# Four operand differences of the last layer: from VectorE to ScalarE sign changes and adding transfers of GpSimd's queue

## The chip, the cores and the metric

The kernel runs on one core of one Trainium2 chip. The metric is the device time in microseconds (us) of one execution, the median of several runs. Engines are named as in the profile: PE is TensorE, DVE is VectorE, ACT is ScalarE, POOL is GpSimd, SP is SyncE, which issues most transfers.

## The reference, cut to what matters

Attention with a tanh cap, then a gated layer (silu), then a second layer with two matrices and a leaky activation. The change lies in the last matrix product.

```
attn = softmax(cap * tanh(q k^T / 8 / cap));  x = attn v      # 2 x 12 heads, 448 rows, 64 wide
xn  = x / rms(x) * rms_g
x   = (silu(xn @ w_gate) * (xn @ w_val)) @ w_out               # 768 -> 1536 -> 768
h   = x @ w_in                                                  # 768 -> 2048
g   = max(h, 0) + alpha * min(h, 0)
out = g @ w_out2                                                # 2048 -> 768, 896 tokens
```

## The kernel before, in words

Every fp32 product is made of three passes over split operands: a number is its rounded high part plus a rest, and PE multiplies high by high, high by low and low by high. A high part is a CAST on ACT (line 133 for weights, line 1187 for the last layer's operands), a low part a subtraction on DVE (line 139 for weights, line 619 through the helper `tt` for operands).

The layers run as blocks of 2 x 2 matrices with Winograd's seven products in place of eight, so that sums and differences of blocks are needed on both sides. In the last layer the inner dimension of 2048 is cut in two. The first half (8 pieces `fh`, `fl`) is multiplied plainly, by the units `c`. The second half is a 2 x 2 block matrix with the quarters B11, B12 (in the buffer `zt[2]`, printed as `b_3496`) and B21, B22 (`zt[3]`, printed as `b_3669`), and goes through the seven products of `LONG`, by the units `f`. Four of its operands are differences, each made in place, in two halves h = 0 and 1 of 128 x 896 elements:

- T1 = B12 - B11, in the place of B11, the operand of product P5;
- T2 = B22 - T1, in the place of T1, the operand of P6;
- T3 = B22 - B12, in the place of B12, the operand of P7;
- T4 = B21 - T2, in the place of T2, the operand of P4.

PE's work is a list of slots of 18 matmuls each. From `f0`, the first slot of the last layer, they are: 8 slots of `c`, then two slots each of P1, P5, P6, P7, P4, then 8 slots of `c` for the other half of the output rows, then two slots each of P3 and P2. So P5 has the slots 10 and 11 after f0, P6 12 and 13, P7 14 and 15, P4 16 and 17; the first slot of a product uses half 0 of its operand, the second half 1. PSUM holds two banks of sums: P1 and P6 write the pair of tiles printed x and m, P5 and P7 the pair printed s.

All work of other engines hangs on slots: `do(n, rank, fn, ...)` puts it behind slot n, and `rank` orders it there. That gives the order of each engine's instructions and no time: an engine runs ahead as far as its waits allow. ACT and DVE run here about one slot ahead of the slot that their work is hung on. Per slot there is a weight unit's high part on ACT (rank 0) and its low part on DVE (rank 2), hung two slots before its use. Its buffer is one of four (`wh`, `wl`), so ACT's cast of a unit waits until PE is through with the unit four before. The raw weights come by SP's queue, three buffers in turn; the next load goes out when DVE has combined (line 118) what came before.

`fsplit` (line 1187) makes the high part of an operand half on ACT, `fsplit_low` its rest on DVE, and `t_sum` a difference on DVE. `keep` (line 1225) copies PSUM sums to SBUF on ACT and `plus` adds them on DVE. The tables that hang all of these on slots are

```
for n, (p, b, at_) in enumerate(zip(LONG, (B11, B11, B11, B12, B11, B22, B21), (4, 7, 10, 12, 14, 20, 22))):
for n, abc in ((6, (B11, B12, B11)), (9, (B11, B22, B11)), (11, (B12, B22, B12)), (12, (B11, B21, B11))):
```

Every operand half goes through the same places: a difference, its high part, its rest, then PE.

Of the kernel before, what the change touches and what calls it, by code (L numbers as in the profile page):

```python
# [13 lines left out]
AF = mybir.ActivationFunctionType  # L14
ALU = mybir.AluOpType
# [42 lines left out]
def attn_moe_kernel(ctx: ExitStack, tc: tile.TileContext, units, qk_in, v, sel, w, gvec, alpha, out):  # L58
    nc = tc.nc
# [354 lines left out]
    with tc.manual_schedule():  # L414
# [203 lines left out]
        def tt(out, a, b, op):  # L618
            nc.vector.tensor_tensor(out=out, in0=a, in1=b, op=op)  # L619
# [70 lines left out]
        def do(n, rank, fn, *a):  # L690
            hooks.setdefault(n, []).append((rank, len(hooks[n]) if n in hooks else 0, fn, a))
# [65 lines left out]
        LONG = ("P1", "P5", "P6", "P7", "P4", "P3", "P2")  # L757
# [125 lines left out]
        f0 = at_of["c", 0, 0, 0]  # L883
# [45 lines left out]
        for g in range(G1):  # L929
            at_ = {p: at_of.get(("g", g, p)) for p in STEADY}  # L930
# [209 lines left out]
        for g in range(G2):  # L1140
            at_ = {p: at_of["z", g, p] for p in STEADY}
# [31 lines left out]
        for k in range(KC):  # L1173
            n = f0 + (-3, -3, -2, -2, 0, 0, 2, 2)[k]
# [3 lines left out]
        B11, B12, B21, B22 = ((2, 0), (2, 1), (3, 0), (3, 1))  # L1178

        def quarter(b, h):  # L1180
            c = b[1] + 4 * h
            return zt[b[0]][:, c:c + 3:2]
# [8 lines left out]
            ls[h] = place(14 + n % 2 * 4 + h)  # L1191
            tt(ls[h], quarter(b, h), hs[h], ALU.subtract)

        def t_sum(out, a, b, h):
            tt(quarter(out, h), quarter(a, h), quarter(b, h), ALU.subtract)

        for n, (p, b, at_) in enumerate(zip(LONG, (B11, B11, B11, B12, B11, B22, B21), (4, 7, 10, 12, 14, 20, 22))):
            for h in range(2):
                do(f0 + at_ + h, 5, fsplit, n, p, b, h)
                do(f0 + at_ + 1 + h, 2, fsplit_low, n, p, b, h)  # L1200
        for n, abc in ((6, (B11, B12, B11)), (9, (B11, B22, B11)), (11, (B12, B22, B12)), (12, (B11, B21, B11))):
            for h in range(2):
                do(f0 + n, 3.5, t_sum, *abc, h)

        def parts_of(i):
            return (fb[i][0][:, :, :S], slice(0, 2)), (fb[i][1][:, :1, :S], slice(2, 3))
# [139 lines left out]
```

## Time and profile before

| what | value |
|---|---|
| median of 3 runs | 552.24 us (552.23 to 552.39) |
| the profiled execution's own time | 552.85 us |
| its span | 551.1 us |
| PE busy | 545.6 us, 99% of the span |
| DVE, ACT, POOL busy | 448.5, 370.6, 98.8 us |
| last layer, from f0 to PE's last matmul | 438.24 to 547.46 us |

The span is what the trace covers, 1.75 us less than the execution's own time. A start time in the rows below is counted from the start of the span. Ends of matmuls are modelled, so PE's row of busy time says that it is fed, not that it is at its peak.

### The profile page before, as it was taken

The numbers are of one execution on the slowest core, as the hardware profiler recorded it, in microseconds if no ns is written. First come the engines' busy times: TensorE is split into PE (matmuls) and PEld (weight loads), VectorE is DVE, ScalarE is ACT, GpSimd is POOL, SyncE is SP. The second block draws the span as 40 slices with busy tenths as digits, with TensorE's granted clock in tenths as the row PEclk, the third lists the DMA queues.
The fourth block names the chain that finished last, engine by engine and source line by source line (L and its number), as shares of the span: only waits on it lengthen the run. The fifth ranks groups of instructions, "written<-read, shape, count | busy, mean of one in ns | idle before, by whom it ended". The sixth has DMA issues, their size and how long they took to land.

```text
span 551.1 us, 7691 instructions
## 1 busy us (share of the span) xinstructions
PE 545.6 (99%) x3061; PEld 461.3 (84%) x3061; DVE 448.5 (81%) x511; ACT 370.6 (67%) x433; POOL 98.8 (18%) x54
## 2 busy tenths in 40 slices
PE   8999999999999999999999999999999999999997
PEld 5444544699999999999999999999999999999996
DVE  4698889898999967878889898979866899999242
ACT  7989999477766554576757554787967996467110
POOL 0034663300065231010000048101111000000000
PEclk9999999999999999999999999999999999999999
DMA  7756420400334534065510573005512267013022
GB/s 253 260 188 197 164 73 8 163 12 1 120 120 162 178 110 171 1 228 173 184 46 1 229 230 114 1 0 173 172 58 69 105 203 255 0 59 115 0 101 100
DMA packets 17316, 66.09 MB, mean 120 GB/s; under 512 B 3584, under 2 KB 5504, under 8 KB 17280
## 3 DMA queue, kind: packets, MB, share of 16 engines
q1 hardware_dynamic: 16746, 65.08, 34.9%
q8 instruction: 24, 0.39, 0.3%
q10 hardware_dynamic: 390, 0.39, 0.2%
q0 software_dynamic: 144, 0.13, 0.1%
q14 instruction: 12, 0.10, 0.1%
HBM read 62.66 MB, written 2.75 MB: 119 GB/s over the span
## 4 chain that ended last, share of the span: by engine, by line
PE 96%; DVE 1%; ACT 1%; DMA 1%; issue 0%; DVEq 0%
PE s L395 19%; PE x L395 13%; PE m L395 13%; PE s L775 9%; PE s L749 8%; PE x L775 7%; PE oo L236 6%; PE s L207 5%; PE x L749 4%; PE m L775 4%; PE rps L249 3%; PE m L749 2%; PE s L408 1%; PE m L408 1%; PE x L408 1%; ACT pt L221 1%
## 5 line engine op out<-in xcount | busy, mean ns | idle before, releaser
L133 ACT CAST wh<-wt 128x768 fp32r<-128x768 f32 x105 | 87.1, 832 | 66.4 <-PE s L775 24.9
L139 DVE TENSOR_TENSOR wl<-wt,wh 128x768 fp32r<-128x768 f32 x108 | 113.6, 1053 | 12.5 <-ACT wh L133 12.2
L126 POOL TENSOR_TENSOR wt<-wt 128x768 f32<-128x768 f32 x33 | 75.1, 2284 | 265.9 <-DVE wt L118 97.9
L113 ACT CAST top<-raw 128x768 f16<-128x768 bf16 x64 | 68.8, 1076 | 27.0 <-DMA raw<-w_in 11.7
L118 DVE SCALAR_TENSOR_TENSOR wt<-raw,top 128x768 uint32<-128x768 uint32 x68 | 69.8, 1028 | 1.5 <-ACT top L113 1.5
L395 PE MATMUL s<-xx,wh 128*128 128x448 f32 x264 | 63.5, 364 | 0.0
L395 PEld LDWEIGHTS s<-xx,wh 128*128 128x128 f32 x264 | 49.4, 187 | 4.6 <-issue 0.7
L395 PE MATMUL x<-xx,wh 128*128 128x448 f32 x204 | 49.9, 366 | 0.0
L395 PE MATMUL m<-xx,wh 128*128 128x448 f32 x204 | 49.5, 364 | 0.0
L619 DVE TENSOR_TENSOR xx<-b,xx 128x896 fp32r<-128x896 f32 (+1 forms) x40 | 48.8, 1228 | 0.6 <-ACT xx L632 0.6
L216 ACT ACTIVATE pt<-s,cinv 128x896 f32<-128x896 f32 (+1 forms) x48 | 41.1, 911 | 6.2 <-PE s L207 5.9
L395 PEld LDWEIGHTS x<-xx,wh 128*128 128x128 f32 x204 | 38.2, 188 | 3.5 <-issue 0.4
L395 PEld LDWEIGHTS m<-xx,wh 128*128 128x128 f32 x204 | 38.2, 187 | 3.0
L775 PE MATMUL s<-xx,wh 128*128 128x448 f32 x132 | 40.0, 362 | 0.0
L236 PE MATMUL oo<-pt,vt 128*32 128x448 f32 x384 | 38.5, 540 | 0.4 <-ACT pt L221 0.3
L221 ACT ACTIVATE pt<-pt,cap_t 128x3136 f32<-128x3136 f32 (+2 forms) x13 | 35.3, 2714 | 0.4
L395 PE MATMUL s<-xx,wl 128*128 128x448 f32 x132 | 33.8, 364 | 0.0
L236 PEld LDWEIGHTS oo<-pt,vt 128*32 128x32 f32 x384 | 12.2, 110 | 23.6 <-issue 21.4
L775 PE MATMUL x<-xx,wh 128*128 128x448 f32 x104 | 31.2, 362 | 0.0
L749 PE MATMUL s<-xx,wh 128*128 128x448 f32 x96 | 27.2, 364 | 0.0
L775 PEld LDWEIGHTS s<-xx,wh 128*128 128x128 f32 x132 | 24.7, 187 | 2.1
L775 PE MATMUL s<-xx,wl 128*128 128x448 f32 x72 | 26.5, 367 | 0.0
(223 smaller groups left out, 1119.0 us busy)
## 6 DMA issues: line engine op xcount, KB each, us to landing
raw<-w_in SPq DMA_DIRECT2D x68, 768.0 KB
rw<-qk_in SPq DMA_DIRECT2D x11, 480.0 KB
vt<-v_in SPq DMA_DIRECT2D x12, 256.0 KB
out<-b SPq DMA_DIRECT2D x2, 448.0 KB
out<-b SPq DMA_DIRECT2D x2, 224.0 KB
out<-e SPq DMA_DIRECT2D x1, 448.0 KB
out<-c SPq DMA_DIRECT2D x2, 224.0 KB
gt<-us SPq DMA_DIRECT2D x23, 3.5 KB
```

The source lines that it names most:

```text
L113: copy(top_of[u].bitcast(F16)[:, 1::2], raw_t[u].bitcast(BF16)[:, 4:4 * n + 4:4])
L118: nc.vector.scalar_tensor_tensor(out=f_t[u].bitcast(U32), in0=raw_t.pop(u).bitcast(U32)[:, 1:2 * n + 1:2], scalar=13, in1=top_of.pop(u), o ...
L126: add(out=t, in0=f_t[a], in1=f_t[b], op=op)
L133: copy(h_t[u], f_t[u].rearrange("p (k m) -> p k m", m=P))
L139: nc.vector.tensor_tensor(out=l_t[u], in0=f_t[u].rearrange("p (k m) -> p k m", m=P), in1=h_t[u], op=ALU.subtract)
L216: nc.scalar.activation(out=t[:, 2 * g:2 * g + w], in_=st.pop((i, g))[:, :w, :S], func=AF.Tanh, scale=cinv)
L221: nc.scalar.activation(out=t[:, done:to], in_=t[:, done:to], func=AF.Exp, scale=cap_t)
L236: nc.tensor.matmul(oo[i][q * Q:q * Q + Q, :S], vv[:, n, q % 2 * Q:q % 2 * Q + Q], t[:, min(n, TILES - 1), :], start=c == 0, stop=c == TG, ...
L395: nc.tensor.matmul(ps[:, r, c0:c1], lhs, rhs[:, c0:c1], start=first and n == 0, stop=n == len(mm) - 1, skip_group_check=True,)
L619: nc.vector.tensor_tensor(out=out, in0=a, in1=b, op=op)
L749: nc.tensor.matmul(dst[m], wt[:, kk * MB + m, :], x, start=first and u == 0 and kk == 0 and n == 0, stop=u == 1 and kk == 1 and n == 2, sk ...
L775: nc.tensor.matmul(dst[m], wt[:, kk * MB + m, :], x, start=start and ks + kk == 0 and i == 0, stop=fin and last and kk == 1 and i == 2, sk ...
```

## The change

The function that makes a difference no longer subtracts on DVE. ACT changes the sign of the quarter in place, and a transfer of POOL's queue adds the other quarter to it in SBUF. The order of operations is changed with it: T3 is made before T2, the halves of T2 and T4 are hung on two slots in turn, and the splits of P5 and P6 are hung one slot later, P6's at a low rank.

```
-        def t_sum(out, a, b, h):
-            tt(quarter(out, h), quarter(a, h), quarter(b, h), ALU.subtract)
-
-        for n, (p, b, at_) in enumerate(zip(LONG, (B11, B11, B11, B12, B11, B22, B21), (4, 7, 10, 12, 14, 20, 22))):
+        def t_sum(b, a, h):
+            q = quarter(b, h)
+            nc.scalar.activation(out=q, in_=q, func=AF.Copy, scale=-1.0)
+            nc.gpsimd.dma_start(out=q, in_=quarter(a, h), accum_op=ALU.add)
+
+        for n, (p, b, at_) in enumerate(zip(LONG, (B11, B11, B11, B12, B11, B22, B21), (4, 8, 11, 12, 14, 20, 22))):
             for h in range(2):
-                do(f0 + at_ + h, 5, fsplit, n, p, b, h)
-                do(f0 + at_ + 1 + h, 2, fsplit_low, n, p, b, h)
-        for n, abc in ((6, (B11, B12, B11)), (9, (B11, B22, B11)), (11, (B12, B22, B12)), (12, (B11, B21, B11))):
+                do(f0 + at_ + h, 5 if p != "P6" else 0.7, fsplit, n, p, b, h)
+                do(f0 + at_ + (p != "P6") + h, 2, fsplit_low, n, p, b, h)
+        for n, step, b, a in ((6, 0, B11, B12), (8, 0, B12, B22), (9, 1, B11, B22), (12, 1, B11, B21)):
             for h in range(2):
-                do(f0 + n, 3.5, t_sum, *abc, h)
+                do(f0 + n + step * h, 3.5, t_sum, b, a, h)
```

On ACT, from the copies of the first `c` sums (slot 6, tiles x and m) to the copies of P5's sums (`e`), the order before is:

```order
L1225 COPY c_4122<-x 128x896
L1225 COPY c_4123<-m 128x448
L133 CAST wh<-wt 128x768
L1187 CAST xx<-b_3496 128x896
L133 CAST wh<-wt 128x768
L1225 COPY b_4172<-s 128x896
L1225 COPY b_4172<-s 128x448
L133 CAST wh<-wt 128x768
L1187 CAST xx<-b_3496 128x896
L133 CAST wh<-wt 128x768
L1187 CAST xx<-b_3496 128x896
L133 CAST wh<-wt 128x768
```

In the changed kernel the same stretch of ACT, after the same copies, is (line 1196 is the sign change; the first pair is of T3, the single ones are the halves of T2; line 1187 makes the high parts, here of P5's two halves and P6's first):

```order
L1196 ACTIVATE b_3496<-b_3496 128x2x448 x2
L1187 CAST xx<-b_3496 128x896
L133 CAST wh<-wt 128x768
L1227 COPY b_4175<-s 128x896
L1227 COPY b_4175<-s 128x448
L1196 ACTIVATE b_3496<-b_3496 128x2x448
L1187 CAST xx<-b_3496 128x896
L133 CAST wh<-wt 128x768
L1196 ACTIVATE b_3496<-b_3496 128x2x448
L133 CAST wh<-wt 128x768
L1187 CAST xx<-b_3496 128x896
L133 CAST wh<-wt 128x768
```

Four sign changes have come into the stretch, and P5's high parts stand behind T3's sign changes. T1's two sign changes stand earlier, before the copies.

On DVE the piece from P1's second low part (the first row) to P5's second low part reads as follows before, with T1's difference as the row `x2` of b_3496 alone:

```order
L619 TENSOR_TENSOR xx<-b_3496,xx 128x896
L118 SCALAR_TENSOR_TENSOR wt<-raw,top_94 128x768
L619 TENSOR_TENSOR b_3496<-b_3496 128x2x448 x2
L139 TENSOR_TENSOR wl<-wt,wh 128x768
L118 SCALAR_TENSOR_TENSOR wt<-raw,top_95 128x768
L126 TENSOR_TENSOR wt<-wt 128x768
L139 TENSOR_TENSOR wl<-wt,wh 128x768
L619 TENSOR_TENSOR xx<-b_3496,xx 128x896
L126 TENSOR_TENSOR wt<-wt 128x768
L139 TENSOR_TENSOR wl<-wt,wh 128x768
L619 TENSOR_TENSOR xx<-b_3496,xx 128x896
```

In the changed kernel the same piece of DVE, from the same row, is:

```order
L619 TENSOR_TENSOR xx<-b_3496,xx 128x896
L118 SCALAR_TENSOR_TENSOR wt<-raw,top_94 128x768
L139 TENSOR_TENSOR wl<-wt,wh 128x768
L118 SCALAR_TENSOR_TENSOR wt<-raw,top_95 128x768
L126 TENSOR_TENSOR wt<-wt 128x768
L139 TENSOR_TENSOR wl<-wt,wh 128x768
L126 TENSOR_TENSOR wt<-wt 128x768
L139 TENSOR_TENSOR wl<-wt,wh 128x768
L619 TENSOR_TENSOR xx<-b_3496,xx 128x896
L126 TENSOR_TENSOR wt<-wt 128x768
L139 TENSOR_TENSOR wl<-wt,wh 128x768
L619 TENSOR_TENSOR xx<-b_3496,xx 128x896
```

The difference is gone, and P5's low parts stand one weight unit later than before: each now stands behind the low part of a unit (line 139) that it stood ahead of.

## Rows read from the trace of the kernel before

**Rows 1.** Busy time by stretch: us; then PE, PEld, DVE, ACT, POOL, granted clock, DMA.

```profile
460.00:470.00 10.00, 10.00 (x51) 9.28 (x50) 9.79 (x12) 7.52 (x10) 0.00 (x0) 1.00 0.51 175
470.00:480.00 10.00, 10.00 (x51) 9.26 (x51) 10.00 (x13) 4.20 (x5) 0.00 (x0) 1.00 0.00 0
480.00:490.00 10.00, 10.00 (x51) 9.28 (x50) 10.00 (x12) 7.29 (x10) 0.00 (x0) 1.00 0.01 2
```

**Rows 2.** Chain that ended last, in order of time: start, us, what.

```profile
474.64 7.28 PE s L775 x36
481.92 1.21 PE x L775 x6
...
485.56 2.43 PE x L775 x12
...
540.16 7.29 PE s L775 x36
547.46 0.02 issue
547.48 0.39 DVE c L619
```

**Rows 3.** Timeline of DVE: start, us, line, operation, tiles.

```profile
458.38 1.09 DVE L619 TENSOR_TENSOR xx<-b,xx 128x896 fp32r<-128x896 f32 x1
459.38 0.95 DVE L118 SCALAR_TENSOR_TENSOR wt<-raw,top 128x768 uint32<-128x768 uint32 x1
460.25 2.09 DVE L619 TENSOR_TENSOR b<-b 128x896 f32<-128x896 f32 x2
462.25 0.95 DVE L139 TENSOR_TENSOR wl<-wt,wh 128x768 fp32r<-128x768 f32 x1
...
474.55 1.08 DVE L619 TENSOR_TENSOR c<-x,c 128x896 f32<-128x896 f32 x1
475.55 0.62 DVE L619 TENSOR_TENSOR c<-m,c 128x448 f32<-128x448 f32 x1
...
476.95 1.08 DVE L619 TENSOR_TENSOR xx<-b,xx 128x896 fp32r<-128x896 f32 x1
...
481.69 1.08 DVE L619 TENSOR_TENSOR xx<-b,xx 128x896 fp32r<-128x896 f32 x1
```

**Rows 4.** Timeline of ACT, the idle time before a row and its releaser in brackets.

```profile
443.97 0.94 ACT L1126 ACTIVATE zn<-b 128x896 f32<-128x896 f32 x1
...
457.37 1.08 ACT L113 CAST top<-raw 128x768 f16<-128x768 bf16 x1
460.42 0.83 ACT L133 CAST wh<-wt 128x768 fp32r<-128x768 f32 x1 [1.97 <-DVE wt L118]
...
462.10 0.94 ACT L1187 CAST xx<-b 128x896 fp32r<-128x896 f32 x1
...
467.19 0.84 ACT L133 CAST wh<-wt 128x768 fp32r<-128x768 f32 x1 [1.33 <-PE s L775]
467.93 1.33 ACT L1225 COPY b<-s 128x896 f32<-128x896 f32 x2
```

**Rows 5.** Timeline of SP's queue: issue of one weight load.

```profile
460.36 0.33 SPq L102 DMA_DIRECT2D raw<-w_in  x1
```

**Rows 6.** Busy time by us in which that load moves; columns as in rows 1.

```profile
461.00:462.00 1.00, 1.00 (x7) 0.93 (x6) 1.00 (x2) 1.00 (x2) 0.00 (x0) 1.00 0.83 123
462.00:463.00 1.00, 1.00 (x7) 0.92 (x6) 1.00 (x2) 1.00 (x3) 0.00 (x0) 1.00 0.87 338
463.00:464.00 1.00, 1.00 (x7) 0.93 (x6) 1.00 (x2) 1.00 (x3) 0.00 (x0) 1.00 0.77 320
```

**Rows 7.** DMA issues: line, count, KB each, median us to landing.

```profile
raw<-w_in SPq DMA_DIRECT2D x68, 768.0 KB
...
sel_t<-sel_in POOLq DMA_DIRECT2D x1, 128.0 KB, 4.8
```

**Rows 8.** Timeline of POOL: its only transfer.

```profile
1.22 0.72 POOL L436 DMA_DIRECT2D sel_t<-sel_in  x1 [0.78 <-POOLq L1336]
```

## The prediction

> **What bounds the kernel now.** I read first the busy time by stretch, to see which engine leaves no gap. In the 30 us in which the four differences are made, PE is busy 10.00 of every 10 us and its granted clock is 1.00; DVE has 9.79 to 10.00, ACT 4.20 to 7.52, POOL nothing, and the DMA engines are idle from 470 on [rows 1]. Next I read the chain that ended last, in order of time: from P5's first slot at 474.64 it is matmuls without a break, slot behind slot of 3.64 us (P5's 36 matmuls take 7.28), to 547.46, and then DVE's last sums and the output [rows 2]. So PE bounds, and a full DVE beside it costs nothing as long as operands come in time. A matmul is not slowed by DVE either: the last 36, at 540.16, with DVE nearly out of work, take 7.29 us against 7.28 for the 36 at 474.64 [rows 2].
>
> From this follows the sign: work taken from DVE here can give next to nothing, while an operand that comes late stops PE and is paid in full. The question is the slack of the operands. Before, P6's low parts end at 476.95 + 1.08 = 478.03 and 481.69 + 1.08 = 482.77 [rows 3]; its slots start at 481.92 and 485.56 [rows 2]. That is 3.9 and 2.8 us, and 3.64 us is one slot.
>
> **The change, part by part.** Removed from DVE: eight subtractions, of which two take 2.09 us [rows 3], so 8 x 1.04 = 8.4 us. DVE is not the bound: 0 us at the end of the program. Added to ACT: eight sign changes. The nearest row is an ACTIVATE of the same 128 x 896, 0.94 us [rows 4], so 7.5 us. ACT has 2.5 us and more idle in each 10 [rows 1], so by itself 0 as well. Added to POOL's queue: eight transfers of 448 KB. POOL has no other work then, so nothing is queued behind them there. What can cost is the time that each transfer stands between two steps of a chain.
>
> The chain starts with T1. Its first sign change can follow ACT's cast at 457.37 + 1.08 = 458.45 and ends at 459.4. The second overwrites what P1's second low part reads, which ends at 458.38 + 1.09 = 459.47, so it ends at 460.4. Before, ACT sat idle 1.97 us there, until 460.42 [rows 3, 4]; this is hidden.
>
> Call X the time at which T1's second half has landed. ACT's next step is T3's sign changes, in place on B12, which T1's transfers read: they have to wait for these, half by half. Behind the second on ACT stand P5's first high part, a weight cast, a copy of sums, T2's sign change and the rest. From rows of 0.94 (sign change, and high part), 0.84 (weight cast), 0.95 (a unit's low part on DVE) and 1.08 (an operand's) [rows 3, 4]: T3's second sign change, P5's first high part and the cast are through at X + 2.7. DVE's low part of that unit and P5's low part: X + 4.75. T2's first sign change: X + 5.7. P5's second high part and a cast: X + 7.5. DVE again two low parts: X + 9.5. T2's second sign change: X + 10.4. DVE meanwhile has a weight sum (0.95), P1's two sums (1.08 and 0.62 [rows 3]), one unit's low part (0.95) and then P6's first low part (1.08): X + 14.2. Rows that follow each other on an engine overlap by 0.08 us (459.38 + 0.95 is 460.33, and the next starts at 460.25 [rows 3]); for about ten of them that is 0.8, so X + 13.4. PE needs that part one matmul, 0.20 us (7.28 / 36), after 481.92. **No stall as long as X is at most 482.1 - 13.4 = 468.7.** P6's second half: sign change done at X + 10, transfer, high part and low part (2.0), needed at 485.8; with 4.2 us for a transfer by itself (below) that allows X = 469.6. T4's halves have some two us more, and weights are cast three slots ahead, so the first limit decides.
>
> Now X. The trace has no adding transfer and none from SBUF to SBUF. Nearest row: a weight load of 768 KB. One issued at 460.36 moves in the next three us, with 0.83 + 0.87 + 0.77 = 2.5 us of all DMA engines [rows 5 to 7]. By its bytes 448 KB takes 1.44 us if the added operand is all that counts, and 2.9 if goal and operand are both read. POOL's row for a transfer is 0.72 us [rows 8], and the load starts some 0.6 us after its issue [rows 5, 6], so a transfer alone takes 2.8 to 4.2 us. T1's pair doesn't move alone: it starts at 459.4 + 0.72 + 0.6 = 460.7, and that load and the one behind it move in the same stretch (175 GB/s over 10 us from 460 is 1.75 MB, two loads and a rest [rows 1]). With half of the engines each, a pair of 2.9 us lands at 460.7 + 5.8 = 466.5; a pair of 5.8 us, last after both loads, at 460.7 + 5.8 + 5.0 = 471.5. The outer ends are a pair at the load's rate with nobody beside it, X = 463.6, and the other transfer of POOL's queue, 128 KB in 4.8 us [rows 7], taken by its bytes: 3.5 x 4.8 = 16.8 us for one, which puts X at 494 and some 25 us on the program. I hold to the load, whose size is nearer, since the 128 KB are loaded in the program's first us together with the first operands. Between 466.5 and 471.5 I take the middle, X = 469.0, so 0.3 us of stall, with 0 and 2.8 as its ends.
>
> The page "Collectives: The Full Stack" of the Trainium skill, section "The bandwidth ceiling: the fold count and why AG ≠ RS ≠ AR", says that an adding transfer is slower because it has two sources to read through one ring, not because of the addition (measured ratio 1.93). No run here shows it yet; by it the pair would take 5.6 us and X be about 471.3, the first rival's case.
>
> **The sum.** The profiled execution took 552.85, its span 551.1. Minus 8.4 on DVE and plus 7.5 on ACT count 0, since PE's row has no gap for either; the stall adds 0.3: 553.15 for an execution like the profiled one, which lies 0.6 above the median of 552.24. For the median: 552.24 + 0.3 = **552.5 us**. A difference under about 0.2%, 1.1 us, can't be told from none here, so this is "the same".
>
> **Rivals.**
> First, slower by two reads beside the loads: X = 471.5. T3's and P5's parts follow it at once, P6's first low part is through at 484.9 against 482.1, and PE stalls 2.8 us before P6's first slot: 555.0. For it: the DMA engines are busy there half of the 10 us, and more in the us of a load [rows 1, 6]. Against it: they have the other half, and two queues may fill each other's gaps. It decides from X = 469.8 on, which is 1.1 us of stall.
> Second, an addition that is slower still, 4.4 us a transfer, half again as long as two reads. X is then about 460.7 + 8.8 + 2.5 = 472.0, T3's pair holds the ring until 480.8, T2's first half lands at 485.5 and P6 starts at 487.5, 5.4 late; its second half adds 0.7. 558.3. For it: 4.8 us for only 128 KB [rows 7]. Against it: the place and company of that row.
> Third, POOL can't write a transfer's description while DVE works: DVE has no gap from 470 to 490 and 0.21 us in the ten before [rows 1]. If every transfer of T1 waits for one row of DVE's more, 1.1 us, X is 471.2 and the time 554.7. Against it: DVE's rows here are all of two inputs [rows 3], and none is a copy.
> On this the Trainium skill, page "SBUF — State Buffer", section "SBUF: two separate sides", warns that a transfer of GpSimd's queue starves while VectorE runs an operation in a two-port mode, as a plain fp32 copy is. This case's rows are no copies, so by that rule there would be no such wait and the chance of this rival is small.
> Fourth, faster: a freer DVE lets something move up. PE has no wait in the stretch [rows 1], so I can name only what lies outside my reading; it would have to be 1.3 us, 550.9.
>
> **Chances.** Same as forecast, X up to 469.8: 0.52. First rival 0.25, second 0.15, third 0.05, fourth 0.03. So faster 0.03, same 0.52, slower 0.45. The likeliest case alone reaches from 551.9 to 553.4. The range has to take in the first and third rivals whole and most of the second, whose upper end is open: 551.9 to 558.3, which leaves out about 0.1 above and a little below.
>
> **What would show it.** POOL has eight transfers of line 1197; the first two land together near 469, and single ones take 3 to 4.5 us. ACT's idle time before T3's sign changes is put down to such a transfer, about 3 us. DVE loses its eight rows and shows idle time instead, waiting for ACT. PE's chain either stays whole from 474.64 to 547.46, or has one gap, right at P6's first slot. A second gap, at P6's second slot or at P4, would mean that a transfer alone is longer than 4.2 us. A pair that lands before 467 refutes the reading of two reads; a gap at P5, or one in which PE waits for a weight unit, refutes the chain as I wrote it. The forecast is wrong if X is beyond 469.8, or if PE stops for anything else.

## The result, and the profile after

The changed kernel takes 556.5 us in the median (555.92 to 558.19, 4 runs), the kernel before 552.27 in the same measurement: ratio 1.0081, 95% interval 1.0059 to 1.0103. It is 4.2 us slower. The profiled execution took 556.65 us with a span of 554.9, against 552.85 and 551.1 for the profiled one before, so between these two the loss is 3.8 us.

PE no longer runs through. These are all of its rows in the last layer that had to wait, in the timeline of PE (start, duration, operation; idle time before it and its releaser in brackets):

```profile
474.99 0.47 PE L775 MATMUL s<-xx,wh 128*128 128x448 f32 x1 [0.41 <-ACT b L1227]
476.19 0.47 PE L775 MATMUL s<-xx,wh 128*128 128x448 f32 x1 [0.73 <-DVE xx L619]
480.79 0.47 PE L775 MATMUL s<-xx,wh 128*128 128x448 f32 x1 [0.69 <-DVE xx L619]
485.06 0.47 PE L775 MATMUL x<-xx,wh 128*128 128x448 f32 x1 [0.36 <-DVE xx L619]
489.29 0.47 PE L775 MATMUL x<-xx,wh 128*128 128x448 f32 x1 [0.32 <-DVE xx L619]
```

Two fall at the start of P5 (the first for ACT's copy of the sums that P5's bank still held, which stands behind T3's late sign change in ACT's order, the second for P5's low part), then one each in P5's second, P6's first and P6's second slot. P6's second slot should pass its second matmul at 485.56 + 0.20 = 485.76 [rows 2] and does so at 489.29, 3.5 us late; with the slower restarts (the row of a matmul behind a wait is 0.47 us, the mean is 0.20) PE's last matmul ends at 551.26 against 547.46 [rows 2], 3.8 us. Each gap is short because the one before has already moved PE back: it is one chain that runs late and PE that is held to it.

The chain of waits of the changed kernel shows that chain; it leaves PE for two stretches of transfer (columns as in rows 2):

```profile
460.74 10.86 DMA b<-b
...
471.64 0.83 issue
472.48 0.93 ACT xx L1187
473.40 0.74 ACT wh L133
...
475.04 1.10 DVE xx L619
...
476.23 0.95 ACT b L1196
477.18 0.83 ACT xx L1187
478.01 0.74 ACT wh L133
...
479.65 1.10 DVE xx L619
...
480.83 0.97 ACT b L1196
481.79 0.35 issue
482.14 5.00 DMA b<-b
...
487.17 0.95 ACT xx L1187
488.12 0.02 issue
488.15 1.10 DVE xx L619
489.25 0.04 issue
489.29 2.49 PE x L775 x11
```

T1's second half takes 10.86 us from issue (the start of POOL's row) to landing, at 471.60. Then come T3's sign change, P5's first half, T2's first sign change, P5's second half, T2's second, one more transfer of 5.00 us and P6's second half. ACT's timeline shows the two waits for T1, one for each half; the weight cast of the first row stands between the copies and T3's sign changes, where the order list above leaves it out:

```profile
464.12 0.84 ACT L133 CAST wh<-wt 128x768 fp32r<-128x768 f32 x1
467.93 0.95 ACT L1196 ACTIVATE b<-b 128x896 f32<-128x896 f32 x1 [2.97 <-DMA b<-b]
471.62 0.95 ACT L1196 ACTIVATE b<-b 128x896 f32<-128x896 f32 x1 [2.74 <-DMA b<-b]
```

DVE, freed of 8.4 us, spends them and more in waiting: from 460 to 490 it is idle for 13.2 us against 0.2 before. 7.34 of them are one wait for ACT's weight cast, which stands behind these rows in ACT's order:

```profile
474.17 0.96 DVE L139 TENSOR_TENSOR wl<-wt,wh 128x768 fp32r<-128x768 f32 x1 [7.34 <-ACT wh L133]
```

The busy time by stretch, which answers to [rows 1], says the same: in the first ten us DVE falls from 9.79 to 4.96 and the DMA engines rise from 0.51 to 0.94.

```profile
460.00:470.00 10.00, 10.00 (x52) 9.27 (x51) 4.96 (x6) 5.30 (x7) 2.73 (x3) 1.00 0.94 240
470.00:480.00 10.00, 8.86 (x42) 7.38 (x40) 4.06 (x5) 6.27 (x8) 2.82 (x3) 1.00 0.73 124
480.00:490.00 10.00, 8.62 (x40) 7.27 (x40) 7.83 (x9) 7.32 (x10) 1.82 (x2) 1.00 0.48 80
```

One transfer by itself (T2's first half, 448 KB) costs 0.78 + 1.13 + 0.85 = 2.76 us of all DMA engines; the last two columns are their share, which is over 1 where the times of packets overlap, and GB/s:

```profile
479.00:480.00 1.00, 1.00 (x6) 0.68 (x4) 1.00 (x2) 0.00 (x0) 0.00 (x0) 1.00 0.78 131
480.00:481.00 1.00, 0.31 (x2) 0.21 (x2) 1.00 (x2) 0.17 (x1) 0.00 (x0) 1.00 1.13 190
481.00:482.00 1.00, 1.00 (x6) 0.93 (x6) 1.00 (x2) 1.00 (x2) 0.00 (x0) 1.00 0.85 138
```

Its row among the DMA issues (KB each, median us to landing), beside [rows 7], and POOL's row for it, 1.2 us where the plain transfer of [rows 8] took 0.72:

```profile
b<-b POOLq DMA_DIRECT2D x8, 448.0 KB, 4.8
```

```profile
477.54 1.21 POOL L1197 DMA_DIRECT2D b<-b  x1 [3.37 <-ACT b L1196]
```

### The profile page after: what moved, and what is told of

Same layout as the page of the kernel before. It is cut to its first block, busy times and chain, and to the rows that moved or that the text cites. A ratio compares the mean times of both kernels' runs of the same rounds, so it can differ in the third digit from the quotient of the medians.

```text
span 554.9 us, 7708 instructions
## 1 busy us (share of the span) xinstructions
PE 546.8 (99%) x3061; PEld 460.7 (83%) x3061; DVE 441.6 (80%) x503; ACT 377.7 (68%) x441; POOL 108.4 (20%) x62
## 4 chain that ended last, share of the span: by engine, by line
PE 86%; DVE 6%; DMA 3%; ACT 3%; issue 2%; POOL 0%; DVEq 0%; ACTq 0%; POOLq 0%
PE s L395 18%; PE x L395 13%; PE m L395 12%; PE s L749 8%; PE oo L236 6%; PE s L775 5%; PE s L207 5%; PE x L749 4%; PE x L775 4%; PE rps L249 3%; DMA b<-b 3%; PE m L749 2%; PE m L775 2%; PE s L408 1%; DVE xx L619 1%
## 5 line engine op out<-in xcount | busy, mean ns | idle before, releaser
L395 PE MATMUL s<-xx,wl 128*128 128x448 f32 x132 | 33.8, 364 | 0.0
L395 PEld LDWEIGHTS s<-xx,wl 128*128 128x128 f32 x132 | 24.7, 187 | 1.9
```

The source lines that it names most:

```text
L395: nc.tensor.matmul(ps[:, r, c0:c1], lhs, rhs[:, c0:c1], start=first and n == 0, stop=n == len(mm) - 1, skip_group_check=True,)
```

## The experiments

Theory A: all of the loss comes from T1's pair of transfers, which read two operands each and share the DMA engines with two weight loads. B: a transfer of 4.8 us is too long in this chain wherever it stands. C: the sign changes on ACT and the new order cost by themselves. Every time below is a median, beside that of the kernel before on the same chip, with the ratio and its 95% interval. PE reaches P5 between 473.7 and 474.6 of the span in different executions, so landings are also given as time before P5's first slot: 471.6 in the changed kernel is 3.0 us before the 474.64 at which that slot was due.

**The addition on VectorE (e1).**

```
-            nc.gpsimd.dma_start(out=q, in_=quarter(a, h), accum_op=ALU.add)
+            tt(q, q, quarter(a, h), ALU.add)
```

> The changed kernel with the sign changes on ScalarE and its whole order, but the addition on VectorE in place of the transfer. Theory A (T1's pair of transfers, which read two operands each and share the DMA engines with two weight loads, lands at 471.6, and all the lateness comes from there): no transfer, so no stall, 552.3 us, PE's chain whole from 474.64 to 547.46. Theory C (the sign changes on ScalarE and the operands split a slot later cost by themselves): 554 to 556.5 with gaps before P5 and P6.

552.63 against 552.46, ratio 1.0004 (0.9995 to 1.0012). No row of PE waits. C falls: ACT's 7.5 us and the later splits are free. DVE still has eight operations here, so this run says nothing of what they cost.

**T1 alone back on VectorE (e2).** T2, T3 and T4 stay as the change makes them.

```
-                do(f0 + n + step * h, 3.5, t_sum, b, a, h)
+                do(f0 + n + step * h, 3.5, t_dve if n == 6 else t_sum, b, a, h)   # t_dve: the subtraction by tt
```

> The changed kernel with only T1's two halves made on VectorE by a subtraction, as before; T2, T3 and T4 by transfers. Theory A: nothing stands before P5, T3's pair now meets the weight loads but P7 needs it only at 489, and T2's single transfers of 4.8 us have room: 552.3, at most 552.8. Theory B (a transfer of 4.8 us by itself is too long in the chain from T1 to T2 to T4, wherever it stands): gaps before P6 stay, 554 to 556.

552.46 against 552.46, ratio 1.0000 (0.9991 to 1.0009), and no row of PE waits. Six of the eight transfers cost nothing. B falls: what a transfer costs depends on where it stands.

**Only T1 by transfers (e7).** The same edit the other way round (`t_sum if n == 6 else t_dve`).

> The changed kernel with only T1's halves by transfers; T2, T3 and T4 by subtractions on VectorE, at their new places in the order. Theory A: T1's second half lands at 469 to 471.6 beside the two loads, T3's subtraction waits for it on VectorE, P5's first low part comes 1 to 2.5 us late and that gap is all: 553.3 to 554.8, some half of the loss; the other half comes from T2's transfers, that start late. If the first pair alone decided all, 556; if T2's transfers alone did, 552.3.

555.24 against 552.14, ratio 1.0057 (1.0044 to 1.0069): 3.1 us, more than I expected. T3's and T2's subtractions wait on DVE in turn, and all that stands behind them in DVE's order waits too, so the gap is not left at P5:

```profile
474.93 0.47 PE L775 MATMUL s<-xx,wh 128*128 128x448 f32 x1 [0.80 <-DVE xx L619]
...
484.19 0.48 PE L775 MATMUL x<-xx,wh 128*128 128x448 f32 x1 [1.49 <-DVE xx L619]
```

T1's second half takes 10.92 us to land, as in the changed kernel, with no other transfer behind it. With e2, in which the other six cost nothing, this leaves T1's pair as the cause. The 3.1 us aren't simply a part of the 4.2, since the lateness goes another way here, through DVE's order. That the rest of the loss is what T2's transfers add when they start late is my reading of the chain of waits above; no run has it alone.

**The two weight loads later (e4).** They go out from ACT's queue, in its order behind T4's first sign change (hung on slot 12); the trace has them issued from 482.07 on. The queue is handed on by `w_next` and `w_load`, which is not shown.

```
+            if u in (("f", 1, "A11"), ("f", 1, "A22")):
+                do(n, 3, w_bits, u)
+                do(f0 + 12, 4.5, w_next, u, nc.scalar)
+            else:
                 do(n, 3, bits, u)
```

> The changed kernel with the two weight loads that move beside T1's pair (issued at 460.3 and 463.2) issued later, from ScalarE's queue, behind T4's first sign change; their weights are cast only from 490 on. Theory A: T1's pair alone lands near 467, under the limit of 468.1 to 468.7 that the chain allows: 552.3 to 553. Theory B: the loads do not matter, 555 to 556.5. If the two reads are most of it and the loads little, T1's second half lands at 470 or later and the time is 555.

552.61 against 552.46, ratio 1.0004 (0.9996 to 1.0013). T1's second half now lands at 466.8, 6.6 us after its issue in place of 10.86, and only this one row of PE waits, before P4, where the late loads meet T4's pair:

```profile
496.56 0.47 PE L775 MATMUL x<-xx,wh 128*128 128x448 f32 x1 [0.48 <-DVE xx L619]
```

**The loads behind P4's first half (e10).** As the last, with slot 14 and rank 5.5, and the next load ordered behind them.

> As e4, but the two weight loads are issued later still, behind P4's first high part, where T4's first half has landed. Theory A: the gap of 0.48 us that e4 has before P4 (T4's pair beside the loads, 8.5 us to land) goes, PE's chain is whole, 552.2 to 552.5, the same as the kernel before and not faster, since PE had no gap to give back. Rival: the late loads hold up weight units and a gap opens behind P4, 552.8 or more.

552.38 against 552.44, ratio 1.0001 (0.9993 to 1.0010). No row of PE waits. ACT's timeline has the landing of T1's second half at 466.38, and the chain has P5 whole at 474.04, 7.7 us later:

```profile
466.38 0.95 ACT L1200 ACTIVATE b<-b 128x896 f32<-128x896 f32 x1 [1.10 <-DMA b<-b]
```

```profile
474.04 7.28 PE s L775 x36
```

This is the best form with all eight transfers that I found. It equals the kernel before and doesn't beat it.

**Only the second load later (e8).**

> As e4, but only the second of the two weight loads is issued later; the first still moves beside T1's pair. Theory A with engine time that adds up: the pair has 5.5 us of engine time and the load 2.5, so T1's second half is 2 to 2.5 us earlier than in the changed kernel and 2 to 2.5 later than in e4: lands near 469 to 469.5, PE stalls 0.8 to 1.8 us, 553.1 to 554.1. If one load is hidden in the gaps of the other queue: 552.3 to 552.6; if the first load alone makes the delay: 555.5 to 556.5.

554.65 against 552.44, ratio 1.0043 (1.0031 to 1.0055): half of the loss, a little over what I expected. The runs lie in two groups, four at 554.11 to 554.76 and two at 556.07 and 556.39. The profiled one is of the second group: T1's second half lands at 471.2 there, 10.85 us after its issue, as long as with two loads, although the engines' work is mostly done by 469. Busy time by us, the DMA share being the number before the last:

```profile
468.00:469.00 1.00, 1.00 (x7) 0.93 (x6) 0.00 (x0) 0.01 (x1) 0.00 (x0) 1.00 0.87 152
469.00:470.00 1.00, 1.00 (x7) 0.93 (x6) 0.00 (x0) 0.94 (x1) 0.00 (x0) 1.00 0.15 27
470.00:471.00 1.00, 1.00 (x7) 0.92 (x6) 0.00 (x0) 0.00 (x0) 0.75 (x1) 1.00 0.09 16
```

A share of 0.15 and 0.09 is the work of one to three engines of sixteen. The packet records of the trace agree that these are late ones on which the transfer's end waits: some 18 packets of POOL's queue are in flight at a time from 468.0 to 468.5, two or three from 469.1 to 470.5, and the last ends at 470.91. No record names the engines, and why a run falls in one group or the other stays open.

**T3 later (e3)**, behind P6's first high part, so that P5's first half need not wait for T1's second. The line that hangs `t_sum` takes `rank` in place of 3.5, which is not shown.

```
-        for n, step, b, a in ((6, 0, B11, B12), (8, 0, B12, B22), (9, 1, B11, B22), (12, 1, B11, B21)):
+        for n, rank, step, b, a in ((6, 3.5, 0, B11, B12), (11, 0.8, 0, B12, B22), (9, 3.5, 1, B11, B22), (12, 3.5, 1, B11, B21)):
```

> The changed kernel with T3's sign changes and transfers hung behind P6's first high part, so that P5's first high part waits for T1's first half alone and T2's transfers have no other ahead of them. Theory A: P5's first half is in time (T1's first half landed at 467.9 in the changed kernel), T2's first half is issued near 473 and lands near 478; one small gap at most at P6: 552.3 to 553.3. Theory B: the chain from T1 to T2 is the same number of transfers, 555 to 556.5.

554.73 against 552.46, ratio 1.0048 (1.0031 to 1.0066). The six runs lie between 553.67 and 557.17; the profiled one took 554.2. In it the gaps at P5 and P6 are gone, as A has it, but I had missed P7, whose first half now comes late:

```profile
490.18 0.47 PE L775 MATMUL s<-xx,wh 128*128 128x448 f32 x1 [1.40 <-DVE xx L619]
```

T2's second half, T3's pair and T4's first half stand close behind each other there; the median landing is 6.5 us in place of 4.8.

**T3 later and the loads later (e6)**, both edits together.

> The edits of e3 (T3 later) and e4 (two weight loads later) together. Theory A: slack on both sides, PE's chain whole, 552.3, equal to the kernel before; it cannot be faster, as PE has no gap there. Theory B: 554 to 556.

555.11 against 552.14, ratio 1.0055 (1.0041 to 1.0069). This is a miss of mine, worse than the loads later alone, and no better than T3 later alone, as the intervals overlap. Now T3's pair meets the two loads, and one transfer takes 12.34 us in the chain. P7 and P4 wait:

```profile
494.55 0.47 PE L775 MATMUL s<-xx,wh 128*128 128x448 f32 x1 [2.26 <-DVE xx L619]
498.82 0.47 PE L775 MATMUL x<-xx,wh 128*128 128x448 f32 x1 [0.36 <-DVE xx L619]
```

It says the same as the changed kernel: loads beside a pair are the harm, at T3 as at T1.

**Plain copies (e5).** The transfers copy and do not add, so this kernel's operands are not differences.

```
-            nc.gpsimd.dma_start(out=q, in_=quarter(a, h), accum_op=ALU.add)
+            nc.gpsimd.dma_start(out=q, in_=quarter(a, h))
```

> The changed kernel with the eight transfers as plain copies: the addition is left out, so the operands are not differences. If reading two operands is what makes a transfer long (theory A): a single one takes 3.3 to 3.8 us from issue to landing in place of 4.8, the DMA engines are busy 1.4 to 1.6 us for it in place of 2.8, T1's second half lands near 467, 552.3 to 553. If it is the writing of the description and the landing on GpSimd's queue: 4.5 or more for a single one, T1's second half at 470 or later, 555 to 556.5.

552.46 against 552.14, ratio 1.0006 (0.9998 to 1.0015), with both loads in place. T1's second half lands at 467.52, 6.4 us before P5's slot at 473.90. The median copy takes 3.0 us to land, POOL's row for it is 0.72, and a copy by itself (T2's second half) costs the engines 0.78 + 0.44 = 1.22 us, in the us that answer to the three of the adding transfer above:

```profile
479.00:480.00 1.00, 1.00 (x6) 0.93 (x5) 1.00 (x3) 0.99 (x2) 0.00 (x0) 1.00 0.78 296
480.00:481.00 1.00, 1.00 (x6) 0.94 (x5) 1.00 (x2) 0.91 (x1) 0.00 (x0) 1.00 0.44 163
```

So the loss needs both: the addition, which makes a transfer 2.76 / 1.22 = 2.3 times as long on the engines, and the loads. The packet records show that this isn't a matter of packet size: the copy is cut into packets of up to 5376 bytes, the adding transfer into packets of 1792, but packets of 1792 bytes take 0.074 us in the one (median) and 0.171 in the other. The loads hold up a plain copy as well: T1's second half takes 7.4 us from issue (460.06) to landing, but the slack covers that. POOL's row is shorter here too, and the pair gets ahead of the first load by it, so what this run takes away with the addition is engine time, POOL's time and that order together.

## Why the prediction was right or wrong

**The bound held, and the range by its width.** PE had nothing to gain: of the four kernels in which it runs through again (e1, e2, e5, e10), none is measurably faster. ACT's 7.5 us were worth 0, shown by e1, and so were DVE's 8.4, shown by e10, in which DVE is free of them. The time lies within the range, 551.9 to 558.3, because the range took in the rivals; the forecast of 552.5 itself was 4 us too low, and by the prediction's own sign, X beyond 469.8, it was wrong.

**The likeliest case was wrong, and the first rival came.** The step that failed is "between 466.5 and 471.5 I take the middle", X = 469.0. X was 471.6; the first rival had 471.5, by two reads of 2.9 us a transfer and all of the two loads added up. Measured are 2.76 us of engine time for a transfer, and with two loads the landing is where that sum puts it; with one load it was nearly as late in the slower group of runs, so the sum is not the whole rule. The middle takes it that the pair and the loads share the engines in part; the packet records show that the pair waits for the first load instead. In the changed kernel that load is issued at 460.29, POOL's row for T1's first half ends at 460.71, and the first packet of data in POOL's queue moves only at 463.69, 3.0 us later; in e8, with this load alone, it is 3.2 us, and in e4, without it, 0.6. From 466.9 on T1's second half moves beside the second load. In e5 POOL's row is shorter, and the first packet moves at 460.16, before that load; whether an adding pair issued half a us earlier would go ahead of it too wasn't tried. A middle between two mechanisms is the place of neither: rows 1 and 6 showed engines that were busy during a load, and a second read had a reason that the trace could not speak against. The first rival should have had the larger chance, but that its X came within 0.1 us is in part luck: in e8 the same sum misses.

**The rival's size was off by 1.0 us of 3.8, and its place as well.** The loss between the two profiled executions is 3.8, the rival's stall 2.8. I put one gap before P6. My own chain, X + 4.75, already makes P5's first low part late at X = 471.5 (476.2 against 474.84), and P5 did wait: that low part ended at 475.04 + 1.09 = 476.13. I held the chain against P6's first slot alone, and a gap at P5 was my own sign that the chain as I wrote it is refuted. That slot came 2.9 us late by the rows above (485.06 against 482.12), as worked out. The last half-slot decides the end, and there the transfer by itself was mis-sized: 4.2 us against 0.35 + 5.00 from the end of the sign change to landing, of which POOL's row is 1.2 and not 0.72. With it X + 10 + 5.35 + 2.0 is 489.0; PE went on at 489.29. The second gap there is the sign that I had named for a transfer of more than 4.2 us.

**The chain's other steps held.** X + 2.7, 4.75, 5.7, 7.5, 9.5 and 10.4, taken from 471.6 and less the overlap, meet the rows of the chain of waits within 0.3 us: P5's first low part ends at X + 4.5, T2's sign changes at X + 5.6 and X + 10.2. T1's sign changes were hidden, T4's halves had room, no weight unit was late.

**The other rivals.** The second, an addition of 4.4 us on the engines, falls at 2.76. Its sum had two slips: it counts one load (2.5) where the first rival counts two (5.0), and 480.8 + 4.4 gives 485.2 where it has 485.5. The third, POOL held off by DVE, falls: POOL's rows are 1.20 to 1.22 us, and start 0.35 to 0.38 us behind the end of the sign change, whether DVE is full (482.14) or idle (472.95). That agrees with the page "SBUF — State Buffer" of the Trainium skill, section "SBUF: two separate sides", which warns of VectorE's two-port modes, as of a plain fp32 copy: DVE's rows in this stretch are no copies and all of two inputs. The fourth did not come. On the first, the page "Collectives: The Full Stack" of the Trainium skill, section "The bandwidth ceiling: the fold count and why AG ≠ RS ≠ AR", gives two source reads as the reason why ReduceScatter is slower than AllGather, and 1.93 as the ratio. Here the ratio is 2.3 on the engines and 4.8 / 3.0 = 1.6 to landing; no run separates a second read from the addition, so that two reads are the reason is not shown.

## What to carry to other kernels

Work taken from an engine that is busy but not the bound gives nothing; a longer way for an operand costs nothing either until its slack is used up, so work out the latest time at which it may land, and hold that against every consumer in the chain, not the one that looked tightest before. For a transfer, ask what else is on the DMA engines when it is issued: six adding transfers here were free, two beside weight loads cost 4 us, and moving the loads (not the transfers) mended it, as long as the loads didn't meet another pair. Where two mechanisms give two landing times, weigh the mechanisms and do not take the middle.

## What the runs showed of the hardware that I had not expected

- An adding transfer of 448 KB within SBUF from GpSimd's queue: POOL 1.20 us, DMA engines 2.76 us, landed after 4.7 to 5.0 us alone. The plain copy: 0.72, 1.22 and 3.0.
- A pair of them beside two weight loads of 768 KB: the second landed 10.9 us after its issue, against 6.2 to 6.6 without the loads (e10, e4). In e6, beside two loads and with a third transfer near, 12.3 us.
- Times scattered more where PE stalled for a transfer: 555.92 to 558.19 in the changed kernel, against 552.23 to 552.39 before in that measurement, and 553.67 to 557.17 in e3. It isn't so in each such kernel (e7 has 555.18 to 555.75), and the cause stays open.
